# A unit of the mixing between products of the channel block, on one core of a Trainium2

## The chip, the core and the metric

The kernel runs on one core of a Trainium2 chip. The metric is the device time of one execution in microseconds; the time of a version is the median of its runs. Engines are named as the profile names them: PE (TensorE, with PEld for its weight loads), DVE (VectorE), ACT (ScalarE), POOL (GpSimd) and SP (SyncE, whose queue issues the DMAs here).

## The reference

Attention with a threshold, then a block that mixes over the sequence and over the channels with a Fourier transform, then a two-layer channel block. All in float32.

```python
# q, k, v: (8 batches, 8 heads, 576, 64); w_ch1: (512, 2048); w_ch2: (2048, 512)
scores = scale * q @ k.transpose(0, 1, 3, 2)
thresh = max(scores, -1) - tau
scores = where(scores >= thresh, scores, -1e9)
attn = exp(scores - max(scores, -1))
attn = attn / (sum(attn, -1) + 1e-9)
x = (attn @ v) with the heads side by side          # (8, 576, 512)
mixed = real(fft(fft(x, axis=1), axis=2))
u = x + mixed
un = (u - mean(u)) / sqrt(var(u) + 1e-6)            # over the channels
out = u + relu(un @ w_ch1) @ w_ch2
```

## The kernel before

**Attention.** A step is 128 queries of a pair of heads. Five steps (t = 0 to 4) make a pair, twenty a batch, 160 in all. `scores` (L433, L444) writes two score tiles `sc` into PSUM. `softmax` takes the row maximum on DVE (`neg`, L461), the exponential on ACT (L469), then threshold and sum on DVE (L477), and divides. `weights_in_parts` transposes the weights of the step before on PE, in parts: a first tile `pe` (L541) and four transposes `pw` (L560), then, after a yield, four more `pw`. ACT copies them out as `ends` (L548) and `e_t` (L562). `weighted_values` multiplies them with v (`pv`, L589) at t=2 and at t=0.

**Mixing.** When a batch's attention is done, `mixing(b)` does its transform as a generator of fourteen units. Three fold rows on DVE and have no matmul (L651 to L682). Six make `py` (L692), even and odd parts in turn, which ACT copies into `y_e` (L697 and a single column, L702) or `y_o`. Five make `pa` (L709, L713): ACT copies the odd part (`tmp`, L724), DVE subtracts and adds (L728, L729), and POOL adds the result to x in `u_t` (L731, L735). Each unit with matmuls counts MIX/11 = 1749.

**Channel block.** The rows of `u_t` go through the two layers in groups of 256 tokens (the first two groups hold 384 and 128). From the third group on, each layer is done with seven products of half-size matrices in place of eight. The generator of a group yields after each piece: in the first layer 4096 (`ph`, L926), in the second 2048 for two of eight 256-column matmuls (`po`, L1090); in the profile each of these matmuls has two records. A product that is done is added into the row tile `u` on DVE (L804). One bank, `sum_`, holds a running sum over five of the seven products of the second layer.

**Order.** For the last 120 steps the program fixes the order of the instructions on PE alone; those of the other engines are put in order when the program is built. After the scores and the softmax of a step come three fills, with the parts of the weights between them:

```python
        next(prep, None)
        fill()
        next(weights, None)
        fill()
        next(weights, None)
        next(prep, None)
        fill()
        next(prep, None)
```

So a step on PE runs: scores, fill, `pe` and four `pw`, fill, four `pw`, fill, and at t=2 or t=0 `pv`. `prep` is there at t=3: it transposes the next pair's q and k (`pq`, `pk`, `pt`).

`fill` (L1169) adds `per_slot`, some 4660, to a budget. If a mixing is under way it takes one unit of it, then units of the channel block until what is spent reaches the budget. `start_batch` sets `per_slot` so that a batch's work lasts for its 60 fills with half a group kept back; this is what stands beside the next mixing.

**PSUM.** All of `pe`, `pw`, `pq`, `pk`, `pt`, `pv`, `py`, `pa`, `pn`, `ph` and `po` (and `sum_`) share four banks (tag "mm"). The score tiles have the other four.

Of the kernel before, what the change touches and what calls it, by code (L numbers as in the profile page):

```python
# [47 lines left out]
def kernel(  # L48
# [607 lines left out]
    MIX = 4 * (3 * 5 * 128 + 5 * 2 * KH)  # L656
# [507 lines left out]
    mixed = 0  # L1164
    work = []
    spent = budget = per_slot = 0.0
    per_batch = NPAIR * NT

    def fill():  # L1169
        nonlocal budget, spent  # L1170
        budget += per_slot
        if mixes:
            mix(1)
        while work and spent < budget and work[0][0] < mixed:
            done = next(work[0][1], None)
            if done is None:
                work.pop(0)
            else:
                spent += done

    total = B * per_batch
    groups = 0
# [123 lines left out]
    def mix(count):  # L1306
        nonlocal spent, mixed
        for _ in range(count):
            done = next(mixes[0], None)
            if done is None:  # L1310
                mixes.pop(0)
                mixed += 1
                break
            spent += done

    def second_batch(i):
# [29 lines left out]
        elif first == 2:  # L1346
            mix(2)
            transposed_weights(i - 1)
            mix(2)
            column_means(LAST)  # L1350
            copy_mean(LAST)
            mirrored(LAST)
            for c, eng in ((1, nc.vector), (3, nc.vector), (0, nc.gpsimd), (2, nc.gpsimd)):
                less_mean(eng, LAST, c)
            weighted_values(n, 0)
            advance(first)
            advance(first)
        else:
            fill()
            transposed_weights(i - 1)  # L1360
            advance(first)
            advance(first)
            fill()
            if t == 3:
                prep_pair(n + 1)
            fill()
            if t == 2:
                weighted_values(n, 0)
            if t == 0:
                weighted_values(n - 1, 1)  # L1370
                folds.append(fold_rows(n - 1))
                load_v(n + 1)
# [96 lines left out]
```

## Time and profile before

| what | value |
|---|---|
| median of 5 runs | 1695.2 us (1694.91 to 1697.52) |
| profiled execution, its own time | 1697.52 us |
| its span | 1695.7 us |
| mean granted clock of PE | 0.994 |
| PE busy | 1635.7 us, 96% |
| PEld busy | 1280.0 us, 75% |
| DVE busy | 1136.9 us, 67% |
| ACT busy | 834.8 us, 49% |
| POOL busy | 585.4 us, 35% |
| first py of the mixings of batches 1 to 7 | 317.0, 531.7, 721.8, 953.9, 1142.3, 1329.3, 1513.0 us |
| matmuls py of even parts, odd parts (records) | 144, 96; median 0.275 us |
| copies of py by ACT, 256 columns | 0.62 to 0.63 us (median) |
| exponential on ACT | 288 x 736 ns |

The span runs from the first instruction's start to the last one's end. A busy PE is not a PE at its peak: a matmul's record is longer than its place in the pipeline, so the distance from start to start is what counts for a row of matmuls. Idle time of an engine that isn't the bound costs nothing by itself. The mixing of batch 0 is done within the second twenty steps, in an order written out by hand; the others are done by `fill`, those of batches 1 to 6 beside the attention of a later batch and that of batch 7 after the last step.

### The profile page before, as it was taken

What the parts mean: (1) busy time and instruction counts of PE and PEld (TensorE: products, weight loads), DVE (VectorE), ACT (ScalarE), POOL (GpSimd) and SP (SyncE); (2) the same over time, 40 slices, a digit from 0 to 9 for tenths busy, and PEclk for the clock granted to TensorE, in tenths of its full rate; (3) what the DMA queues carried; (4) which work ended last, traced back from release to release, by engine and by line L of the source; (5) the groups of instructions that cost most, each with busy time, mean ns of one, the idle gap of its engine ahead of it and who ended that gap; (6) DMA issues with size and microseconds to landing.
All of it is one profiled execution on the core that took longest, in us unless ns stands there. A gap on an engine that the chain in (4) does not pass through costs nothing.

```text
span 1695.7 us, 28896 instructions
## 1 busy us (share of the span) xinstructions
PE 1635.7 (96%) x10838; PEld 1280.0 (75%) x10838; DVE 1136.9 (67%) x2518; ACT 834.8 (49%) x1817; POOL 585.4 (35%) x779
## 2 busy tenths in 40 slices
PE   8998899999999999999999999999999999999998
PEld 4555555566887788878888778886878778789998
DVE  6885886556757586766566757676676758663454
ACT  5764675544555464545354546454646446442111
POOL 5673463040421442134331143223242144124332
PEclk9999999999999999999999999999999999999999
DMA  5323222010010101000101010100001000000000
GB/s 162 112 54 108 72 72 52 23 28 21 15 40 9 34 16 41 22 27 8 28 22 34 8 34 15 41 22 25 25 16 41 20 23 15 14 1 13 14 14 13
DMA packets 130384, 57.48 MB, mean 34 GB/s; under 512 B 121123, under 2 KB 121125, under 8 KB 130246
## 3 DMA queue, kind: packets, MB, share of 16 engines
q1 hardware_dynamic: 128854, 55.35, 12.1%
q8 instruction: 86, 1.41, 0.3%
q10 hardware_dynamic: 1392, 0.30, 0.1%
q14 instruction: 52, 0.43, 0.1%
HBM read 46.02 MB, written 9.44 MB: 33 GB/s over the span
## 4 chain that ended last, share of the span: by engine, by line
PE 76%; DVE 13%; ACT 8%; issue 2%; POOL 2%; DVEq 0%; ACTq 0%; POOLq 0%
PE ph L926 23%; PE po L1090 18%; PE pv L589 9%; PE sc L433 7%; PE pw L560 5%; PE po L848 3%; ACT e L469 3%; DVE neg L461 3%; DVE e L477 3%; PE sc L444 2%; PE py L692 1%; PE ph L822 1%; PE pd L112 1%; DVE hs L1051 1%; DVE f L673 1%
## 5 line engine op out<-in xcount | busy, mean ns | idle before, releaser
L461 DVE TENSOR_REDUCE neg<-sc 128x1 f32<-128x576 f32 x288 | 205.7, 751 | 195.7 <-PE sc L433 184.6
L469 ACT ACTIVATE e<-sc,neg 128x576 f32<-128x576 f32 x288 | 211.8, 736 | 246.8 <-DVE neg L461 246.1
L477 DVE SCALAR_TENSOR_TENSOR e<-sc,thr,e 128x576 f32<-128x576 f32 x288 | 227.2, 814 | 59.5 <-ACT thr L473 58.2
L1090 PE MATMUL po<-w,hs 128*128 128x256 f32 x1024 | 248.8, 386 | 0.3 <-DVE u L804 0.3
L1090 PEld LDWEIGHTS po<-w,hs 128*128 128x128 f32 x1024 | 187.5, 192 | 33.2 <-issue 11.0
L926 PE MATMUL ph<-u_t,w 128*128 128x128 f32 x1536 | 187.5, 276 | 0.2 <-ACT u L788 0.2
L560 PE MATMUL pw<-ident,e 128*128 128x128 f32 x1152 | 171.7, 276 | 13.3 <-ACT ends L552 3.2
L926 PEld LDWEIGHTS ph<-u_t,w 128*128 128x128 f32 x1536 | 178.7, 192 | 4.8 <-issue 3.1
L433 PE MATMUL sc<-kT,qT 64*128 64x288 f32 x1024 | 166.0, 429 | 7.9 <-DVE e L477 7.4
L562 ACT COPY e_t<-pw 128x512 f32<-128x512 f32 x256 | 148.4, 593 | 47.8 <-PE pw L560 46.0
L935 DVE TENSOR_TENSOR hs<-ph,hs 128x512 f32<-128x512 f32 x160 | 107.4, 686 | 79.9 <-PE ph L926 56.6
L560 PEld LDWEIGHTS pw<-ident,e 128*128 128x128 f32 x1152 | 136.2, 142 | 32.6 <-issue 4.9
L433 PEld LDWEIGHTS sc<-kT,qT 64*128 64x128 f32 x1024 | 91.7, 186 | 68.7 <-issue 42.8
L804 DVE SCALAR_TENSOR_TENSOR u<-po,rstd,u 128x256 f32<-128x256 f32 (+1 forms) x164 | 76.3, 483 | 77.2 <-PE po L1090 75.4
L926 PE MATMUL ph<-t_u,s_w 128*128 128x128 f32 x1024 | 126.1, 276 | 1.9 <-ACT ends L548 1.1
L926 PEld LDWEIGHTS ph<-t_u,s_w 128*128 128x128 f32 x1024 | 119.3, 192 | 5.9 <-issue 2.3
L1090 PE MATMUL po<-hs,s_tile 128*128 128x256 f32 x512 | 122.1, 382 | 0.0
L943 ACT ACTIVATE hs<-hs 128x512 f32<-128x512 f32 x112 | 69.3, 629 | 71.0 <-DVE hs L935 70.8
L1090 PEld LDWEIGHTS po<-hs,s_tile 128*128 128x128 f32 x512 | 93.6, 190 | 13.6 <-issue 2.1
L496 ACT ACTIVATE e<-e,den 128x576 f32<-128x576 f32 x96 | 74.4, 775 | 53.3 <-DVE den L489 52.7
L1086 POOL TENSOR_TENSOR hs<-hs,s_tile 128x512 f32<-128x512 f32 x32 | 42.6, 1331 | 125.8 <-PE po L1090 119.8
L492 DVE TENSOR_SCALAR e<-e,den 128x576 f32<-128x576 f32 x120 | 81.2, 677 | 2.6
(199 smaller groups left out, 2881.4 us busy)
## 6 DMA issues: line engine op xcount, KB each, us to landing
hs<-in_moe_w_ch_dram SPq DMA_DIRECT2D x23, 512.0 KB, 4.3
out_dram<-u SPq DMA_DIRECT2D x36, 256.0 KB, 2.2
qk_in<-in_q_dram SPq DMA_DIRECT2D x64, 128.0 KB, 2.2
v_in<-in_v_dram SPq DMA_DIRECT2D x64, 128.0 KB, 2.4
qk_in<-in_k_dram SPq DMA_DIRECT2D x31, 128.0 KB, 2.4
w<-in_moe_w_ch_dram SPq DMA_DIRECT2D x6, 512.0 KB, 7.5
qk_in<-in_k_dram SPq DMA_DIRECT2D x31, 64.0 KB, 2.2
stage<-in_moe_w_ch_dram SPq DMA_DIRECT2D x3, 512.0 KB, 3.8
```

Of the source, the lines that this page charges most:

```text
L433: nc.tensor.matmul(sc[j][:, c, 0:HALF], qT[hp, 128 * t : 128 * t + 128], kT[hp, HALF * c : HALF * (c + 1)], start=True, stop=True,)
L461: nc.vector.tensor_reduce(out=neg[:, j : j + 1], in_=sc[j][:, :, 0:HALF], axis=AXIS_XY, op=ALU.max, negate=True,)
L469: nc.scalar.activation(out=ej, in_=sc[j][:, :, 0:HALF], func=ACT.Exp, bias=neg[:, j : j + 1], scale=1.0)
L477: nc.vector.scalar_tensor_tensor(out=ej, in0=sc[j][:, :, 0:HALF], scalar=thr[:, j : j + 1], in1=ej, op0=ALU.is_ge, op1=ALU.mult, accum_out ...
L492: nc.vector.tensor_scalar(out=e[:, 0:S], in0=e[:, 0:S], scalar1=den[:, 0:1], scalar2=None, op0=ALU.mult)
L560: nc.tensor.transpose(pw[:, c, :], e[:, c0 : c0 + 128], ident[:, :])
L562: nc.scalar.copy(e_t[:, 4 * j : 4 * j + 4, qs], pw[:, :, :])
L589: nc.tensor.matmul(pv[64 * j : 64 * j + 64, 0:m], vt[:, 2 * c + j, :], e_t[:, 4 * j + c, 0:m] if c < 4 else ends[:, 0:m], start=(c == 0), ...
L804: nc.vector.scalar_tensor_tensor(out=u, in0=product, scalar=self.rstd[:, t : t + 1], in1=u, op0=ALU.mult, op1=ALU.add,)
L926: nc.tensor.matmul(banks[name][:, 128 * q : 128 * q + 128], left[c][:, 512 * part + 128 * q : 512 * part + 128 * q + 128], right[c], start ...
L935: nc.vector.tensor_tensor(out=to, in0=bank, in1=to if other is None else other, op=ALU.add)
L1090: nc.tensor.matmul(bank[:, 0 : DM // 2], left[p], right[p], start=start and p == 0, stop=p == NK - 1, skip_group_check=True,)
```

## The change

`fill` gets an inner function, `products(end)`, which holds the loop over the channel block's units as it was, with the bound as its argument. While a mixing is under way, `fill` first runs it up to half of what the fill has left beside a mixing unit, then takes the unit, then runs it up to the whole budget. Without a mixing, `fill` does what it did.

```diff
     def fill():
         nonlocal budget, spent
         budget += per_slot
+
+        def products(end):
+            nonlocal spent
+            while work and spent < end and work[0][0] < mixed:
+                done = next(work[0][1], None)
+                if done is None:
+                    work.pop(0)
+                else:
+                    spent += done
+
         if mixes:
+            products((spent + budget - MIX / 11) / 2)
             mix(1)
-        while work and spent < budget and work[0][0] < mixed:
-            done = next(work[0][1], None)
-            if done is None:
-                work.pop(0)
-            else:
-                spent += done
+        products(budget)
```

## The prediction

> **What bounds the kernel.** I read the page's busy shares first: PE 96%, DVE 67%, ACT 49%, POOL 35%. PE is the bound, so only PE's idle time, or a lower clock, can pay or cost. Next, the waits of PE and the busy rows by window, then the timelines of the seven stretches with a mixing (317, 532, 722, 954, 1142, 1329 and 1513 us; I number them 1 to 7). In each, t is the step's place in its five.
>
> The table of waits: what PE waits for is mostly a PSUM bank of the four under the tag "mm", given back by an ACT copy (columns: who, for whom, us in total, times, longest).
>
> ```profile
> PE py L692 <- ACT ends L548: 5.3, 4, 1.5
> PE pw L560 <- ACT y_e L702: 2.2, 1, 2.2
> PE py L692 <- DVE u L804: 1.2, 1, 1.2
> PE py L692 <- ACT y_e L702: 1.2, 1, 1.2
> ```
>
> Stretch 4, PE and ACT (start, us, engine, line, names, count, idle time before):
>
> ```profile
> 953.86 0.66 PE L692 MATMUL py<-dim_c,f 128*128 128x65 f32 x4
> 954.85 0.49 PE L692 MATMUL py<-dim_c,f 128*128 128x128 f32 x2 [0.33 <-DVE f L673]
> 955.17 1.03 PE L1090 MATMUL po<-w,hs 128*128 128x256 f32 x4
> 956.46 0.33 PE L541 MATMUL pe<-ident,e 128*128 128x128 f32 x1 [0.26 <-DVE u L804]
> 956.63 0.60 PE L560 MATMUL pw<-ident,e 128*128 128x128 f32 x4
> 958.72 0.86 PE L692 MATMUL py<-dim_s,f 128*128 128x128 f32 x4 [1.49 <-ACT ends L548]
> 959.37 1.92 PE L1090 MATMUL po<-w,hs 128*128 128x256 f32 x4
> ...
> 955.37 0.63 ACT L697 COPY y_e<-py 128x256 f32<-128x256 f32 x1 [2.56 <-PE py L692]
> 955.78 0.22 ACT L702 COPY y_e<-py 128x1 f32<-128x1 f32 x1
> 957.77 0.74 ACT L469 ACTIVATE e<-sc,neg 128x576 f32<-128x576 f32 x1 [1.76 <-DVE neg L461]
> 958.40 0.26 ACT L548 COPY ends<-pe 128x128 f32<-128x128 f32 x1
> 958.75 0.74 ACT L469 ACTIVATE e<-sc,neg 128x576 f32<-128x576 f32 x1
> ```
>
> ACT works in order, and its first exp waits until 957.77 for a row maximum that DVE reaches late (the folds of the mixing, L673, are before it). All that stands behind that exp on ACT is late too: here `ends`, which holds the bank that py needs.
>
> The windows show what follows: after that 1.49 us of idle time the same four matmuls of L1090 take 1.92 us instead of 1.03. In stretches 4 and 6 the granted clock falls, in 5 it doesn't (columns: window, its length, PE, PEld, DVE, ACT, POOL busy, clock, DMA).
>
> ```profile
> 953.80:967.40 13.60, 11.52 (x68) 7.83 (x66) 9.39 (x19) 5.52 (x13) 2.13 (x2) 0.87 0.00 0
> 1142.30:1154.30 12.00, 9.92 (x68) 6.69 (x66) 9.58 (x19) 5.70 (x13) 2.45 (x2) 1.00 0.00 0
> 1329.30:1342.90 13.60, 11.53 (x68) 7.86 (x66) 9.36 (x19) 5.52 (x13) 2.09 (x2) 0.87 0.00 1
> ```
>
> **What the change does to the order.** Nothing is added or removed. I worked the budget through by hand: per fill the same units come out in both versions, in another order. The three fold units of a mixing have no matmul. Of the 77 units with matmuls (7 x 11), 55 have only one product unit in their fill (or all of it fits the first half): it now goes first, so the mixing unit lands at the end of its fill, right before pe, pw, pv or the scores. 19 land between products, 3 stay. A mixing unit issues no DMA, and in these fills no output store moves past one, so SP's queue is as it was. POOL's additions to u_t (L731, L735) come some 0.87 us later; their reader, the next group, is units away except in the tail.
>
> A product unit, called P, is four records, 0.865 us start to start (955.17 above is stretched; at 979.99 to 980.85 it is clean; 1.72 in stretch 1, where P is 512 wide). py is 0.65 (six records) or 0.44 (four), pw 0.44.
>
> **A. First two fills of t=2, stretches 4 to 6.** Now: scores, py, P, pe, pw, py, P, pw. Then: scores, P, py, pe, pw, P, py, pw. The scores end at 953.9, P at 954.8, py at 955.4 (the 0.33 us wait for DVE is covered), pe still waits for DVE to 956.46. Then pw finds all four banks taken: the running sum, P's new product, py, pe. The one that ACT frees first lets it go; behind pw stands all of PE in order.
>
> Which is that? ACT's order is fixed at build time and not in the program's text. Today y_e is ready 2.3 us before the exp in the trace and goes first. With py 0.87 us later I expect the exp before it, as the trace has it where py is late against the scores: in stretch 1 y_e comes after both exps, in stretch 2 its small copy (L702) does, and in t=3 of all stretches y_o sits behind the first exp. From the starts in the trace (exp to next 0.64, y_e 0.42, thr 0.18, exp 0.62, small copy 0.22): 957.77 + 0.64 + 0.42 + 0.18 + 0.62 + 0.22 = 959.85, so pw starts at 959.9 instead of 956.63. From there pw, P, py, pw, P, py = 0.44 + 0.87 + 0.44 + 0.44 + 0.87 + 0.65, and two steps of 0.1 between groups: pv starts near 963.7. It started at 963.92 in 4 and 6, and, on the same zero, at 962.30 in 5. That gives -0.2, +1.4, -0.2 = +1.0 at full clock. Half clock cost 963.92 - 962.30 = 1.6 after a gap of 1.49. A gap of 3.3 us (956.6 to 959.9) will bring it each time: +1.0 + 3 x 1.6 = **+5.8**. The other bound is in the second rival (-4.1).
>
> The Trainium skill ("TensorE: Matmul & The Clock Gate", Part 1) says that the clock halves after an idle window of about 3.4 us. Gaps of 1.49 and 2.18 us have halved it here, so the trace disagrees; by the page gaps of 3.3 and 1.8 us might not, A would be +1.0, B +0.7 and the sum -2.4.
>
> **B. Same place, stretch 3** (three P in the fill, two of them before py): py ends at 724.2, exp runs at 724.93 as now, y_e is done at 724.93 + 0.64 + 0.42 + 0.18 + 0.62 + 0.22 = 727.0; pw starts there, not at 725.24. Then pw, P, py, P = 2.6 to the next pw at 729.7, which was 728.97: +0.7, and +1.6 if the gap of 1.8 us lowers the clock. Known gaps: 1.49 (twice of three), 2.18 (once of one). Taken: lowered, **+2.3**; bounds -0.85 and +2.3.
>
> **C. Stretch 2.** pw waits 2.18 us for y_e today (535.74). The product that ends in P now ends 0.65 us earlier, so its bank may come free by 535.4; or y_e is 0.65 later. -0.3 to +0.65, taken **0**.
>
> **D. Stretch 1.** py_o's wait of 1.15 us (321.31, for y_e) lies behind the 1.72 us of P now: next pw at 322.2 instead of 323.57. One product bank less is held there, so pw doesn't wait. **-1.3**; bounds -1.4 and 0 (y_e later by as much).
>
> **E. t=3, stretches 2, 4, 5, 6.** y_o is copied between the exps (968.99). py 0.87 us later puts it behind the second: 968.35 + 0.64 + 0.18 + 0.62 + 0.60 = 970.4, and pw, at 969.80 today, waits for it: +0.6, less 0.25 that py_e lost at 970.49 and P covers. +0.4 each, **+1.6**; bounds 0 (DVE frees the ended product's bank first) and +2.4.
>
> **F. t=4, stretches 4 to 6.** pa waits 0.21 us (0.37 with the restart) for DVE's tmp L729; P now goes first and covers it: **-1.1**; other bound 0.
>
> **G. t=0, stretches 2, 4, 5, 6.** The single-row pa waits for ACT's e_t (0.68, start to start 0.84 lost at 989.03). P covers it: 4 x 0.84 = **-3.3**; other bound -1.5, if pw's wait for `ends` before it (0.62) grows by half.
>
> **H. Tail, stretch 7.** py waits 1.20 us for DVE (1515.94); one more P goes before it: -0.87. At 1540.99 ph waits 0.93 for POOL's last u_t row, whose chain starts after pa. Thirteen P lie between that py and pa in both orders, so POOL ends when it did and the gain goes into that wait. **0**; up to +1.6 if its 1.8 us lowers the clock.
>
> Sum: 5.8 + 2.3 + 0 - 1.3 + 1.6 - 1.1 - 3.3 + 0 = **+4.0**. The profiled execution took 1697.5 (span 1695.7), the slowest of five; I put the sum on the median: 1695.2 + 4.0 = 1699.2.
>
> **Rivals.** (1) The same waits move, but the clock holds: A +1.0, B +0.7, the sum -2.4, so 1692.8. For it: stretch 5 kept its clock through 1.49 us. Against: 2.18 us in stretch 2 did not, and A's gap is longer. (2) The faster side: ACT still takes y_e before the exp. Then pw in A starts at 956.63, P hides behind the wait for `ends`, py starts at 958.72, the next pw waits for e_t (959.37 + 0.59) and pv starts at 962.0: -1.9, -0.3, -1.9 = -4.1; B -0.85, C -0.3, D -1.3, E 0, F -1.1, G -3.3. Together -10.9, 1684.3. It decides at one place: y_e before or after L469 at t=2. For it: 2.3 us of room today, more than 0.87. Against: that room is DVE's lateness on the chip; the order is set ahead, and rows of DVE (neg behind a later-written L1051 at 956.33) show it was set with the scores ending much later against DVE, so the room counted on was small. (3) The change does not do what it says: a unit at the end of a fill, not in its middle. That holds for 55 of 77 whatever the time; it is in every case above.
>
> **Chances.** Forecast 0.50, rival 1 0.20, rival 2 0.25, an order changed elsewhere 0.05. A change under 0.2% (3.4 us) can't be told from none. Forecast: 0.44 slower, 0.06 same (its own range 1696 to 1704). Rival 1: 0.12 same, 0.07 faster, 0.01 slower. Rival 2: 0.24 faster, 0.01 same. The rest slower. Slower 0.50, same 0.19, faster 0.31. The range reaches from 1686 (rival 2 short of its full gain) to 1705 (E and H at their upper bounds: 1699.2 + 0.8 + 1.6, and the rest for C and the runs' own spread of 2.6).
>
> **What would show it.** Right: in stretches 4 to 6 y_e (L697 or L702) behind the exps, a wait of pw for y_e of some 3 us, granted clock below 1 in all three; py's wait for `ends` gone; the t=0 wait for e_t gone. Wrong: y_e before exp at t=2, no wait of pw over 1 us, clock 1.00 in these windows; then rival 2 is what happened.

## The result, and the profile after

| | median (us) | runs | profiled execution (us) | its span | its granted clock |
|---|---|---|---|---|---|
| before | 1696.75 (1694.91 to 1698.96) | 50 | 1697.52 | 1695.7 | 0.994 |
| after | 1700.86 (1696.7 to 1702.38) | 30 | 1698.78 | 1697.0 | 0.993 |

The ratio is 1.0024, with a 95% interval of 1.0019 to 1.0029: the changed kernel is slower by 0.24%, or 4.1 us, where +4.0 was forecast. The two profiled executions lie only 1.2 us apart: the one of after is among the fastest of its runs, the one of before is above its median. So the traces show where time went, but not quite how much of it.

The page of after, its busy shares:

```profile
PE 1632.0 (96%) x10838; PEld 1283.3 (76%) x10838; DVE 1134.1 (67%) x2518; ACT 834.8 (49%) x1817; POOL 582.0 (34%) x779
```

Nothing is to be seen here: the same engines, the same shares, 3.7 us less in PE's records. The next view does show it: the table of PE's waits of after (who, for whom, us in total, times, longest).

```profile
PE pw L560 <- ACT y_e L702: 13.4, 5, 3.0
...
PE pw L560 <- ACT ends L552: 2.7, 4, 0.9
...
PE pw L560 <- ACT y_o L697: 2.6, 5, 0.6
PE pe L541 <- DVE u L804: 2.4, 3, 0.8
...
PE ph L926 <- POOL u_t L731: 1.8, 1, 1.8
```

Gone are py's 5.3 us for `ends` and the waits of the single-row pa for `e_t` at t=0. In their place pw waits 13.4 us, five times, for a copy of one column (L702). It was 2.2 us, once. The timeline of after in stretch 4, from just ahead of the wait, PE and then ACT:

```profile
950.24 1.13 PE L1090 MATMUL po<-w,hs 128*128 128x256 f32 x4
951.20 0.83 PE L692 MATMUL py<-dim_c,f 128*128 128x65 f32 x6
952.84 0.33 PE L541 MATMUL pe<-ident,e 128*128 128x128 f32 x1 [0.81 <-DVE u L804]
956.20 1.11 PE L560 MATMUL pw<-ident,e 128*128 128x128 f32 x4 [3.03 <-ACT y_e L702]
957.11 1.91 PE L1090 MATMUL po<-w,hs 128*128 128x256 f32 x4
...
954.15 0.74 ACT L469 ACTIVATE e<-sc,neg 128x576 f32<-128x576 f32 x1 [4.97 <-DVE neg L461]
954.79 0.60 ACT L697 COPY y_e<-py 128x256 f32<-128x256 f32 x1
955.18 0.29 ACT L473 ACTIVATE thr<-neg,thr_off 128x2 f32<-128x2 f32 x1
955.36 0.74 ACT L469 ACTIVATE e<-sc,neg 128x576 f32<-128x576 f32 x1
955.98 0.16 ACT L702 COPY y_e<-py 128x1 f32<-128x1 f32 x1
956.02 0.29 ACT L548 COPY ends<-pe 128x128 f32<-128x128 f32 x1
```

py is done by 952.1, and ACT has nothing to do for 4.97 us up to 954.15. It still doesn't take the copy of y_e, because the exp (L469) stands ahead of it in ACT's order and waits for `neg`. Between the exps comes the wide copy, behind both the single column that gives py's bank back, and pw starts 0.06 us after it. After the wait the four records of L1090 take 1.91 us instead of 1.03. The windows of stretches 4, 5 and 6 from the scores on (length; PE, PEld, DVE, ACT, POOL busy; granted clock; DMA):

```profile
949.00:966.00 17.00, 13.16 (x82) 10.10 (x81) 10.99 (x23) 6.08 (x15) 2.89 (x2) 0.90 0.00 0
1137.90:1153.50 15.60, 11.76 (x66) 9.31 (x65) 9.78 (x21) 5.55 (x13) 2.88 (x2) 0.78 0.00 0
1327.90:1342.40 14.50, 10.66 (x67) 8.37 (x67) 9.74 (x21) 5.29 (x13) 2.89 (x2) 0.88 0.01 1
```

The clock falls in all three; before it fell in two. From the start of the scores to the start of the next scores these stretches took 13.54, 11.92 and 13.54 us before, and 14.47, 15.58 and 14.49 now.

### The profile page after: what moved, and what is told of

The parts are those of the page before. It is cut to its first block, busy times and chain, and to the rows that moved or that the text cites. A ratio compares the mean times of both kernels' runs of the same rounds, so it can differ in the third digit from the quotient of the medians.

```text
span 1697.0 us, 28905 instructions
## 1 busy us (share of the span) xinstructions
PE 1632.0 (96%) x10838; PEld 1283.3 (76%) x10838; DVE 1134.1 (67%) x2518; ACT 834.8 (49%) x1817; POOL 582.0 (34%) x779
## 4 chain that ended last, share of the span: by engine, by line
PE 77%; DVE 12%; ACT 8%; issue 2%; POOL 1%; DVEq 0%; ACTq 0%
PE ph L926 23%; PE po L1090 18%; PE pv L589 9%; PE sc L433 7%; PE pw L560 6%; PE po L848 3%; ACT e L469 3%; DVE neg L461 2%; DVE e L477 2%; PE sc L444 2%; PE ph L822 1%; PE py L692 1%; DVE hs L1051 1%; PE pd L112 1%; PE pa L709 1%
## 5 line engine op out<-in xcount | busy, mean ns | idle before, releaser
L469 ACT ACTIVATE e<-sc,neg 128x576 f32<-128x576 f32 x288 | 211.9, 736 | 254.8 <-DVE neg L461 254.2
L1090 PE MATMUL po<-w,hs 128*128 128x256 f32 x1024 | 250.8, 387 | 0.4 <-DVE u L804 0.3
L1090 PEld LDWEIGHTS po<-w,hs 128*128 128x128 f32 x1024 | 187.1, 192 | 35.2 <-issue 13.6
L560 PE MATMUL pw<-ident,e 128*128 128x128 f32 x1152 | 172.8, 277 | 25.8 <-ACT y_e L702 13.4
L804 DVE SCALAR_TENSOR_TENSOR u<-po,rstd,u 128x256 f32<-128x256 f32 (+1 forms) x164 | 76.1, 483 | 74.1 <-PE po L1090 72.9
L1090 PE MATMUL po<-hs,s_tile 128*128 128x256 f32 x512 | 123.5, 383 | 0.0
L1090 PEld LDWEIGHTS po<-hs,s_tile 128*128 128x128 f32 x512 | 93.0, 190 | 13.5 <-issue 2.1
L496 ACT ACTIVATE e<-e,den 128x576 f32<-128x576 f32 x96 | 74.4, 775 | 53.6 <-DVE den L489 53.3
L1086 POOL TENSOR_TENSOR hs<-hs,s_tile 128x512 f32<-128x512 f32 x32 | 42.4, 1326 | 127.6 <-PE po L1090 102.7
L731 POOL TENSOR_TENSOR u_t<-x,tmp 128x289 f32<-128x289 f32 (+1 forms) x47 | 35.9, 769 | 139.9 <-DVE tmp L728 122.0
```

Of the source, the lines that this page charges most:

```text
L469: nc.scalar.activation(out=ej, in_=sc[j][:, :, 0:HALF], func=ACT.Exp, bias=neg[:, j : j + 1], scale=1.0)
L496: nc.scalar.activation(out=e[:, S : 2 * S], in_=e[:, S : 2 * S], func=ACT.Copy, scale=den[:, 1:2])
L560: nc.tensor.transpose(pw[:, c, :], e[:, c0 : c0 + 128], ident[:, :])
L804: nc.vector.scalar_tensor_tensor(out=u, in0=product, scalar=self.rstd[:, t : t + 1], in1=u, op0=ALU.mult, op1=ALU.add,)
L1090: nc.tensor.matmul(bank[:, 0 : DM // 2], left[p], right[p], start=start and p == 0, stop=p == NK - 1, skip_group_check=True,)
```

## The experiments

All diffs are against the changed kernel, where none other is named.

**1. Only the later fills of a step.** A step calls `fill` three times; the first lies between the scores and pe. Theory: the loss is in that first fill alone, and the others are gains.

```diff
-    def fill():
+    def fill(part=None):
...
-            products((spent + budget - MIX / 11) / 2)
+            if part in (1, 2):
+                products((spent + budget - MIX / 11) / 2)
...
-        fill()
+        fill(0)
...
-        fill()
+        fill(1)
...
-        fill()
+        fill(2)
```

> The change in the second and third fill of a step alone; in the first fill, and after the last step, the mixing unit goes first as before. Theory (the cost lies in the first fill, where py moves behind the product, its copy goes behind the exponentials on ACT and pw waits for the bank; the later fills gain): no wait of pw for y_e in stretches 4 to 6, the wait of py for ends falls from 1.49 to some 0.6 us, clock 1.00 there, and the time is 1685 to 1688, faster than before and after. Rival (the cost lies in the later fills, where the mixing unit now stands right before pw, pv or the scores): 1700 or more.

Measured: 1683.81 us (1680.28 to 1684.98), ratio to before 0.992 (0.9907 to 0.9934), 1.2 us below the range that was expected. That beats both kernels: by 13.6 us before's 1697.44 in the same call, by 17.1 us the changed kernel. Stretch 4 of this run, PE and then ACT:

```profile
950.83 1.03 PE L1090 MATMUL po<-w,hs 128*128 128x256 f32 x4
952.13 0.33 PE L541 MATMUL pe<-ident,e 128*128 128x128 f32 x1 [0.27 <-DVE u L804]
952.29 0.60 PE L560 MATMUL pw<-ident,e 128*128 128x128 f32 x4
952.73 1.03 PE L1090 MATMUL po<-w,hs 128*128 128x256 f32 x4
954.38 0.71 PE L692 MATMUL py<-dim_s,f 128*128 128x128 f32 x4 [0.62 <-ACT ends L548]
955.68 0.66 PE L560 MATMUL pw<-ident,e 128*128 128x128 f32 x4 [0.59 <-ACT e_t L562]
...
951.03 0.63 ACT L697 COPY y_e<-py 128x256 f32<-128x256 f32 x1 [2.56 <-PE py L692]
951.45 0.21 ACT L702 COPY y_e<-py 128x1 f32<-128x1 f32 x1
953.43 0.74 ACT L469 ACTIVATE e<-sc,neg 128x576 f32<-128x576 f32 x1 [1.77 <-DVE neg L461]
954.07 0.26 ACT L548 COPY ends<-pe 128x128 f32<-128x128 f32 x1
```

y_e is ahead of the exp again, done 1.8 us before it starts. The product of the second fill (952.73) now lies in what was py's wait for `ends`: 0.62 us are left of 1.49, the clock stays at 1.00, and the stretch takes 11.52 us instead of 13.54. Stretches 5 and 6 take 11.53 and 11.52.

**2. Only the first fill.** The other half: `if part in (1, 2)` above becomes `if part == 0`.

> The reverse: the change in the first fill of a step alone, the other fills and the tail as before. Theory: the 3 us wait of pw for y_e and the half clock stay in stretches 4 to 6, the gains at the single-row pa (0.8 us in four stretches), at the pa before it (0.3 in three) and in stretch 1 (1.3 to 1.9) go: 1703 to 1707, slower than the change. Rival (cost in the later fills): about the time of before, 1696 to 1697.

Measured: 1706.51 us (1706.05 to 1709.01), ratio 1.0061 (1.0048 to 1.0074). Its waits begin with the same row as after's:

```profile
PE pw L560 <- ACT y_e L702: 13.4, 5, 3.0
```

The first fill makes the loss and the later ones make the gain, but they don't add up. From the first scores of stretch 1 to the end, against before in the profiled executions, it is +9.9 us here and -12.7 in experiment 1, together -2.8, and +1.4 in after. (Ahead of stretch 1, where these fills have no mixing, this execution took 1.6 us more than before's; that isn't the change.) At t=2 in stretches 3 to 6 the first fill costs 9.5 us alone (15.92, 15.91 and 15.91 us in 4 to 6, 14.45 in 3) and 11.6 beside the later ones (after less experiment 1, in the table below), although the half clock lasted longer here: 6.83 us in each of 4 to 6, in after 3.41, 6.83 and 3.41. py's wait for `ends`, which the later fills cover in experiment 1, is gone here without them, so that part of their gain is not there to be had twice. And the tail's +1.1, further down, is in neither half.

**3. Work for PE in the wait.** Is the price the 3 us of idle time, or the clock after it? Eight matmuls that feed nothing, into the unused half of an open bank, go to PE's order in stretches 4, 5 and 6 after the first fill, ahead of pe.

```diff
+            opened[:] = [bank]
...
+    opened = []
+
+    def beside(n):
+        for _ in range(n):
+            nc.tensor.matmul(
+                opened[0][:, 256:512], ident[:, :], dim_c[:, 1:257],
+                start=False, stop=False, skip_group_check=True,
+            )
...
+        if i in (102, 122, 142):
+            beside(8)
```

> The change, with eight extra matmuls of 256 columns (3.5 us) in the first fill of t=2 of stretches 4 to 6, between py and pe, where PE waits for DVE and then for y_e until some 4.2 us after py; they write into the unused half of the open product's bank, which nothing reads. Theory (the waits let the clock fall, and that is some 1.6 us of each of the three): granted clock 1.00 in the three windows, pv some 1.3 to 2.4 us earlier in each, 1695 to 1697. Rival (the waits alone make the cost; the clock matters little): 1700 to 1701. If the extra matmuls run longer than the wait, up to 1 us more for each stretch.

Measured: 1700.45 us (1699.27 to 1702.05), ratio 1.0021 (1.0012 to 1.003). No gain, the rival's number and not the theory's, though the clock is 1.00 in all three windows. The timeline of stretch 4 in this run says why:

```profile
958.75 0.66 PE L560 MATMUL pw<-ident,e 128*128 128x128 f32 x4 [0.60 <-ACT y_e L702]
...
961.05 0.78 ACT L496 ACTIVATE e<-e,den 128x576 f32<-128x576 f32 x1 [2.18 <-DVE den L489]
961.73 0.57 ACT L562 COPY e_t<-pw 128x512 f32<-128x512 f32 x1
962.35 0.66 PE L560 MATMUL pw<-ident,e 128*128 128x128 f32 x4 [1.63 <-ACT e_t L562]
```

With the extra matmuls ahead of pe, ACT's order has the division (L496) ahead of the copy of `e_t`, and the next pw waits 1.63 us for it. The run changed two things and doesn't decide between the two; experiment 6 puts the matmuls in another place.

**4. The odd parts first.** In the mixing, py for odd parts (four records, no single-column copy behind them) goes ahead of py for even parts. Then the bank that pw waits for comes free with the wide copy.

```diff
-            for odd in range(2):
+            for odd in (1, 0) if b > 0 else (0, 1):
```

> The change, with the odd unit of each pair of py first (mixings of batches 1 to 7). The odd unit has one copy on ACT where the even one has two, and in the trace of the change the second, a single column, goes behind the second exponential in stretches 4 to 6 while the first goes before it. Theory (pw waits for the last copy that reads py's bank): pw starts 0.7 to 0.9 us earlier in stretches 4 to 6, the wait falls from 3.0 to some 2.2 us, 1697.5 to 1699.5. Rival (pw waits for the exponentials or for ends, not for that copy): wait unchanged, 1700 to 1701.

Measured: 1699.54 us (1695.7 to 1702.38), ratio 1.0015 (1.0006 to 1.0024). Stretch 4 of this run:

```profile
955.81 0.68 PE L692 MATMUL py<-dim_s,f 128*128 128x128 f32 x4 [0.78 <-DVE f L682]
...
958.45 0.61 ACT L697 COPY y_o<-py 128x256 f32<-128x256 f32 x1
959.12 0.66 PE L560 MATMUL pw<-ident,e 128*128 128x128 f32 x4 [2.28 <-ACT y_o L697]
```

pw starts 6.38 us after the scores instead of 7.13, and waits for the wide copy, as said. But py of odd parts now waits 0.78 us for DVE's last fold (L682), the clock still falls in all three stretches, and the medians of this run and of after differ by only 1.3 us, with intervals of the ratios that overlap. The bank is confirmed; the remedy brings little.

**5. Only the steps with t=2 put back.** Here the first fill of t=2 alone is as before; all else is the change.

```diff
-    def fill():
+    def fill(late=True):
...
-            products((spent + budget - MIX / 11) / 2)
+            if late:
+                products((spent + budget - MIX / 11) / 2)
...
-        fill()
+        fill(t != 2)
```

> The change, with only the first fill of the steps at t=2 as before (the py with which each mixing beside attention begins, six fills in all). Theory (A and B of the prediction are that one place): the 3 us wait of pw for y_e goes in stretches 4 to 6 and the 1.65 us one in stretch 3, the clock stays up there, the gains of the other fills stay, and so do the losses at t=3 (0.35 us in four stretches) and in the tail (1.1): 1685 to 1688, all but 1 to 4 us of what the second and third fill alone reached (1683.8). Rival (the first fills of t=3, t=4, t=0 share the cost): 1692 or more.

Measured: 1688.17 us (1687.27 to 1688.63), ratio 0.9951 (0.9937 to 0.9965): six calls of `fill` in the whole kernel cost 12.7 us by the two medians, 13.4 with each taken against before in its own call (+4.1 and -9.3). From scores to scores at t=2, in the profiled executions (us):

| stretch | before | after | exp. 1 | exp. 5 | exp. 6 |
|---|---|---|---|---|---|
| 1 | 13.12 | 11.35 | 11.36 | 11.36 | 11.35 |
| 2 | 13.31 | 11.83 | 12.94 | 12.93 | 13.33 |
| 3 | 13.71 | 14.47 | 12.85 | 12.84 | 14.47 |
| 4 | 13.54 | 14.47 | 11.52 | 11.52 | 13.52 |
| 5 | 11.92 | 15.58 | 11.53 | 11.52 | 13.52 |
| 6 | 13.54 | 14.49 | 11.52 | 11.52 | 13.52 |

After less experiment 5 is +10.5 us over these rows, of 11.5 between their spans; the rest lies ahead of stretch 1, where they don't differ. Stretch 2's -1.1 in it is the clock, which fell there in this execution of experiment 5 and not in that of after (see the last section). Experiment 1 is 2.8 us faster still in the profiled executions (4.4 in the medians). At t=3 its stretches 2, 4, 5 and 6 take 0.7 us less each than those of experiment 5, 2.8 in all, at t=4 nothing in sum, and its tail 1.1 less; ahead of stretch 1 its execution took 0.9 more. So the first fill of t=3 costs as well, by little.

**6. The clock once more.** Six of the matmuls of run 3, now between pe and pw, where PE stands anyway.

```diff
-        qs = slice(q0, q0 + (128 if t < 4 else 64))
+        qs = slice(q0, q0 + (128 if t < 4 else 64)); beside(6 if i in (101, 121, 141) else 0)
```

> The change, with six extra matmuls of 256 columns (2.6 us) in the 3.0 us wait between pe and pw, in the first fill's place of t=2 in stretches 4 to 6; the order of ACT is that of the change, which it was not with eight of them before pe (there ACT's division went ahead of the e_t copy and the next pw waited 1.6 us for it). They write into the unused half of the open product's bank. Theory (half clock after the wait is a cost of its own): clock 1.00 in the three windows, pw starts as late as in the change, scores of the next step 1.2 to 2.4 us earlier in each, 1694 to 1697. Rival (the wait is the whole cost): 1700 to 1701.

Measured: 1697.13 us (1695.21 to 1698.3), ratio 1.0 (0.9991 to 1.0009). This time ACT's order is that of after up to the first copy of `e_t`, and pw starts 7.15 us after the scores, as late as in after (7.13). The windows of the three stretches in this run:

```profile
950.00:965.00 15.00, 13.38 (x86) 10.23 (x86) 12.49 (x26) 6.49 (x14) 4.64 (x3) 1.00 0.00 1
1139.00:1154.00 15.00, 13.37 (x88) 9.85 (x88) 11.39 (x22) 6.57 (x15) 3.55 (x3) 1.00 0.00 1
1328.00:1343.00 15.00, 13.38 (x90) 9.86 (x89) 10.77 (x21) 5.48 (x13) 3.18 (x2) 1.00 0.00 1
```

The wait is as long, PE is kept at work in it, the clock holds, and the kernel is 3.7 us faster than the change. So the half clock is a price of its own, apart from the wait: 14.47 - 13.52 = 0.95, 15.58 - 13.52 = 2.06 and 14.49 - 13.52 = 0.97, together 4.0 us.

That is the least of it, for ACT's order is not quite that of after. The division (L496) stands behind y_o and the second `e_t` in after and ahead of them here, and a py waits for y_o. Stretch 4 of this run:

```profile
961.37 0.78 ACT L496 ACTIVATE e<-e,den 128x576 f32<-128x576 f32 x1 [1.01 <-DVE den L489]
962.06 0.61 ACT L697 COPY y_o<-py 128x256 f32<-128x256 f32 x1
...
962.71 0.65 PE L692 MATMUL py<-dim_c,f 128*48 128x65 f32 x6 [0.37 <-ACT y_o L697]
```

This wait is there in each of the three stretches. If all of it comes from the moved division, the half clock costs up to 1.1 us more, 5.1 in all (an estimate). The rest of the cost is the wait: 13.52 against the 11.92 of stretch 5 before, which had no half clock, is 1.6 us in each, of which up to 0.4 is that py's.

**7. Both remedies.** Experiments 1 and 4 together, to take away the one wait for y_e that experiment 1 has left (2.2 us, stretch 2).

> The change in the second and third fill alone, with the odd unit of each pair of py first. It is to take the last long wait of pw for y_e, in stretch 2 (2.2 us, single-column copy behind both exponentials), since the odd unit has no such copy. Theory: pw in stretch 2 starts 2 us earlier, clock there 1.00, and the odd unit waits up to 0.8 us for DVE's last fold in stretches 4 to 6: 1680 to 1683, faster than with the even one first (1683.8). Rival (the odd unit's wait for the fold eats it): 1684 to 1686.

Measured: 1687.2 us, the median of four of its five runs (1684.3 to 1689.8), ratio 0.9944 (0.9931 to 0.9958); the fifth run, at 5742 us, is left unexplained (with it the median is 1688.54). That is above the theory's range and the rival's. The long wait of pw for y_e in stretch 2 is gone, and this row of its waits of PE has come:

```profile
PE py L692 <- DVE f L682: 7.9, 6, 1.8
```

Odd parts need all of DVE's folds, even parts only some; first in line, they wait for them, six times. In the profiled execution the clock falls in stretches 4 and 6 again, and they take 12.33 us where experiment 1 has 11.52. Experiment 1's runs end at 1684.98, so the two remedies together are no gain over the one.

## Why the prediction was right

The likeliest case came true: slower, by the mechanism named, by the amount named (1699.2 on a base of 1695.2, 1700.86 on one of 1696.75). That the amount fits to 0.1 us is luck: the steps are off by up to 1.5 us each, both ways. By its steps, with the shift in each place read from the starts of the scores in the two profiled executions:

| step | predicted | measured |
|---|---|---|
| A, t=2, stretches 4 to 6 | +5.8 | +0.94, +3.67, +0.93 = +5.5 |
| B, t=2, stretch 3 | +2.3 | +0.8 |
| C, t=2, stretch 2 | 0 | -1.5 |
| D, t=2, stretch 1 | -1.3 | -1.8 |
| E, t=3 | +1.6 | 4 x 0.35 = +1.4 |
| F, t=4 | -1.1 | -0.6 |
| G, t=0 | -3.3 | -3.4 |
| H, tail | 0 | +1.1 |
| sum | +4.0 | +1.2 (span), +4.1 (medians) |

**A held.** ACT's order came out as written down: exp, y_e, `thr`, exp, single column. From the exp to pw it was reckoned at 2.13 us (957.77 to 959.9) and took 2.05. The clock fell three times of three. The half clock was set at 3 x 1.6 = 4.8; experiment 6 puts it between 4.0 and 5.1. The change of order at full clock was set at +1.0 (its own terms add up to 963.76, which makes +1.1); experiment 6 against before, 13.52 x 3 - 13.54 - 11.92 - 13.54, is +1.6, or +0.5 if y_o's wait of 0.37 in each is the experiment's own. So both parts were about right, and how far each was off the runs don't tell.

**B and C were mis-sized by the clock.** Their waits came (1.65 us in stretch 3, 2.65 in stretch 2, up from 2.18), and after neither did the clock fall in the profiled execution of after. The same two places in after:

```profile
529.70:541.60 11.90, 9.25 (x68) 6.69 (x67) 7.18 (x18) 5.41 (x13) 1.27 (x1) 1.00 0.01 2
718.00:732.00 14.00, 12.36 (x81) 9.11 (x79) 10.35 (x21) 5.63 (x13) 6.51 (x4) 1.00 0.00 0
```

and stretch 2 before, with the shorter wait:

```profile
531.60:545.00 13.40, 11.22 (x68) 7.99 (x66) 7.13 (x18) 5.73 (x13) 1.27 (x1) 0.87 0.01 2
```

B's 1.6 for the clock was not paid, and the 0.8 that is left is what the step gave for the wait (0.7). In experiments 3 and 6, whose stretch 3 is that of after, it took 14.46 and 14.47 us, with no fall either: this term of the sum should have been nothing. C is a matter of the execution. Experiments 3 and 6 have the same fills and the same wait of 2.65 us in stretch 2 as after; there the clock fell, and the stretch took 13.33 us both times, 0.02 more than before, which is the step's 0. In after's execution it didn't fall and the stretch took 11.83, outside the step's bounds, which left no room for a clock that holds. The last section shows what made the difference. If most runs of after are like those two, these 1.5 us are about half of what lies between the pair of profiles (+1.2) and the medians (+4.1); that, and the rest, stays open. The mean granted clock differs from run to run of after (0.994 in one of 1696.7 us, 0.990 in one of 1702.2).

**D, E, F and G** came in their places, with their signs. D went past its bound (-1.8 against -1.4). F's 0.37 us per stretch is what the later fills alone give (t=4 in stretch 4: 8.30 us before, 7.93 in experiment 1); the first fill takes some of it back (8.14 in after). E was two effects: 0.7 us lost in the first fill, as experiments 1 and 5 differ, and about half of that gained in the later ones.

**H was wrong.** py's wait for DVE's u (L804) did not shrink by 0.87 us, it grew from 1.20 to 1.42 us; and ph's wait for POOL's last u_t row grew from 0.93 to 1.80, as the step said it would. The gain that was to pay for it was not there. The step took DVE's u to come when it did, and it came 1.1 us later: the instruction ahead of it on DVE (L1051, `hs`) took 1.77 us instead of 0.68. In after a POOL addition (L1086) had begun 0.2 us before that L1051, in before it began 0.5 us behind its start. In experiment 1, whose last fills are as before, L1051 takes 0.68 us and the two waits are 1.2 and 0.9 again.

**The rivals.** The first (the clock holds) is refuted at A, true at B, and true at C in after's execution alone. The second (ACT still takes y_e first, 1684.3) did not happen in the change. But its price at t=2 was right: experiment 1 makes its condition true by putting the first fills back, stretches 4 to 6 give -2.0, -0.4 and -2.0 where it had -1.9, -0.3 and -1.9, and stretch 3 gives -0.86 where it had -0.85. That the time, 1683.81, is so near is chance in part: the gain is 13.6 us where it had 10.9, on a base that is 2.2 us higher. What no step of the prediction did was to price the fills of a step apart: the gain and the loss were in different calls and could have been had singly. The third rival holds as it was put (55 of 77 units at the end of their fill), and decides nothing about the time.

The measured answer to "why slower", then: the first fill of the six steps with t=2 puts a product ahead of py, py reaches ACT behind an exp that DVE holds back, and PE, in order and out of PSUM banks, stands 3 us in stretches 4 to 6 for a copy of one column, with a slower clock behind it. That costs 12.7 to 13.4 us. All other fills together gain 9.3 (1688.17 against 1697.42 in the same call).

Open: what the runs of after paid for the clock on average, and a version of experiment 1 that is rid of stretch 2's wait without a new one.

## What to carry to other kernels

A unit that is moved by less than a microsecond on the engine that bounds can change places with a late instruction on another, in-order engine; then it costs the wait of that instruction, not the microsecond, so look, for each operand handed over, at what stands next to it in the receiving engine's order and how late that is. Before an edit that acts in many places is kept or dropped, price and try its places apart: here one call in three lost more than the other two gained, and leaving it out was worth 17 us.

## What the runs showed of the hardware

The clock goes by windows of fixed length. In the nine traces every change of the granted clock lies on a grid of 3.413 us that runs through the whole execution, and a half clock lasts one window of it or, as in stretch 5 of after, two. What goes with a fall is how long PE is idle within one window, by its records. From 240 us on, the nine traces hold 20 windows at full clock with more than 1.84 us idle, and half clock followed all 20; of ten with 1.74 to 1.84, it followed four; of those with less, none. (Ahead of 240 us, in another order of work, it followed six windows with 1.2 to 1.4 us idle, so idle time by the records is not the whole of it.) Four windows of the grid, each with the next one: stretches 4 and 5 of before, stretch 2 of after and stretch 2 of experiment 6 (columns as above; 3.41 less the first busy time is PE's idle time, and the clock of the second row tells whether it fell).

```profile
955.73:959.14 3.41, 1.66 (x11) 1.02 (x10) 3.41 (x7) 1.65 (x6) 0.00 (x0) 1.00 0.00 0
959.14:962.55 3.41, 3.41 (x16) 2.61 (x15) 3.37 (x10) 1.71 (x4) 1.12 (x1) 0.50 0.00 0
...
1143.46:1146.87 3.41, 1.99 (x11) 1.29 (x11) 3.41 (x8) 1.25 (x3) 0.00 (x0) 1.00 0.00 0
1146.87:1150.29 3.42, 3.09 (x21) 2.51 (x22) 3.42 (x9) 3.15 (x9) 1.36 (x1) 1.00 0.00 0
...
532.44:535.85 3.41, 1.59 (x10) 1.33 (x11) 3.41 (x12) 2.46 (x7) 0.00 (x0) 1.00 0.00 0
535.85:539.26 3.41, 3.41 (x30) 2.54 (x31) 1.03 (x3) 2.28 (x5) 1.27 (x1) 1.00 0.02 5
...
533.19:536.60 3.41, 1.05 (x7) 1.00 (x8) 3.41 (x11) 2.52 (x7) 0.00 (x0) 1.00 0.00 0
536.60:540.02 3.42, 3.42 (x14) 3.00 (x13) 1.57 (x4) 1.88 (x4) 0.00 (x0) 0.50 0.02 5
```

So it isn't the length of a gap that counts, as the prediction had it, but how a border of the grid cuts it. The same wait of 2.65 us in stretch 2 is cut by the border at 532.44 in after and lies almost whole in a window in experiment 6. A's two waits (0.81 and 3.03 us, with 0.3 of work between) are so long that, by an estimate from these rows, wherever a border lies one window gets about 1.9 us of them; B's 1.65 never sufficed. One stretch in which the clock fell lost 0.95 to 2.06 us by experiment 6, and at least that. The Trainium skill ("TensorE: Matmul & The Clock Gate", Part 1) puts the fall at an idle window of about 3.4 us and says that the window runs freely, so that the place where it strikes varies. The length of the window and its running freely agree with the grid; but a window need not be idle throughout: 1.75 us of 3.41 was enough in stretch 4 of before.

DVE's L1051 (128x512) took 0.66 to 0.70 us in all of the 204 cases in before and after in which no POOL instruction was under way when it began. Of the 84 in which one was, 54 took more than 1 us, up to 1.82.

Extra matmuls that use nothing of ACT changed ACT's order in both places where they were tried: ahead of pe the division moved ahead of both copies of `e_t` (experiment 3), between pe and pw ahead of the second (experiment 6). What an experiment adds to one engine has to be read off the other engines' orders before its time is believed.
